# Loading and scaling in the front of a fused top-k attention and PReLU-MLP kernel: v cast on the way in, one scaling a tick, w_in turned in pieces

## The chip, the cores and the metric

The kernel runs on one core of one Trainium2 chip. The metric is the device time of one execution in microseconds; the time given for a kernel is the median of its runs. A core has five engines that run side by side, each with its own instruction stream: TensorE (PE, with its weight loads PEld), VectorE (DVE), ScalarE (ACT), GpSimd (POOL) and SyncE (SP, which here issues DMAs only). They wait for one another through semaphores. DMAs are issued by SyncE, GpSimd or ScalarE, in the order of that engine's stream.

## The reference

```python
scores = scale * np.matmul(q, k.transpose(0, 1, 3, 2))          # 8 x 8 heads, 576 x 576, D = 64
kth = np.partition(scores, -32, axis=-1)[..., -32:-31]
scores = np.where(scores >= kth, scores, -1e9)
attn = softmax(scores)                                           # rows
x = (attn @ v) with the heads of a batch side by side            # 4608 x 512
h = x @ w_in                                                     # 512 x 2048
g = np.maximum(h, 0.0) + alpha * np.minimum(h, 0.0)
out = g @ w_out                                                  # 2048 x 512
```

All inputs and the output are float32.

## The kernel before

The work is cut into 32 pairs of heads (a pair shares the 128 partitions) and 288 tiles of 128 query rows by 576 keys, nine tiles to a pair (`TPP = 9`; the ninth holds the last 64 rows of both heads). Tiles are taken singly or two at a time ("units"); the ninth of a pair is a unit of its own.

The order of all instructions is written out by hand in one loop over ticks n (from line 837 of the kernel before; one tile's work per tick on each engine, spread over several ticks). Each tile goes through:

- `scores`: TensorE, q times k in float32 into PSUM (`ps`).
- `act_b`: ScalarE adds a per-row limit `NT0` to the scores (`b`); `act_s`: ScalarE sums the signs of b (`h`, `S_all`), which counts how many scores are over the limit; `act_e`: ScalarE takes the exponential.
- `side_of`: GpSimd turns the count of the tile before into a sign bit `SG`; `flip`: VectorE applies it to b (`y`). The flip of tile n - 1 stands at the end of VectorE's tick n.
- `seg_ops` and `merge_ops`: VectorE finds the largest of six segments of y and merges them (`C`, `L`), from which `sel_*` and `limit` pick the exact limit `KP`.
- `mask` (VectorE, `mk`) and `weights` (GpSimd, `w`), seven ticks behind the scores; then SyncE issues a DMA that turns the weights (`wT`), and TensorE multiplies them with v (`av`, `pu`), after which VectorE takes reciprocals (`av_rz`, `rz`).

On GpSimd a tick is: a possible weight load, the weights product of the tile seven ticks back, then the sign of tile n - 1. On VectorE the mask comes first and the flip last.

`prep_plan(p)` gives each pair its preparation: the turning of q and k by TensorE (`pq`, `pk`, `pt`), their copies out of PSUM by ScalarE, a statistic of the scores (`pg`, `GK`, `pr`, `P`, `st`, `M2`) that ends in `NT0`, and `act_v`, the cast of v from float32 (`st_v`) to bfloat16 (`v_bf`) by ScalarE. For pair 0 it runs ahead of the loop at ticks -16 to -1, for pair 1 at ticks 0 to 9, with VectorE's part `dve_2` waiting for ScalarE's `act_m` at tick 7. `load` and `load_v` issue the loads of q, k and v; `load_v` uses SyncE.

`weight_steps` prepares the MLP beside the first tiles, one step a tick from a queue: alpha is loaded and turned; each 128-row block f of w_out (16 of them) is loaded into one of three staging buffers and scaled twice by ScalarE in one tick, by 1 - alpha into `w_out_b` (line 644) and by alpha into `lin(f)`, which borrows space in `xT` (line 645); w_in is loaded and cast by GpSimd's DMA in four parts kk (`w_in`, two issues each) and each part is turned by one SyncE DMA (`w_in2`, line 636); last, `w_id` multiplies the turned w_in with the scaled w_out (64 products of 128 x 512, line 653), so that the PReLU can be done as a ReLU and one more product. One f takes two ticks; all of it takes ticks 0 to 47. From tick 51 the same queue holds the MLP's own steps.

The pieces of a tick run in this order: the scores of the next unit, what ScalarE still owes from the last step (the scalings), b and h of this tile, one step of the queue, the preparation's TensorE part, then VectorE's and GpSimd's work.

## Time and profile before

| | us |
|---|---|
| median of 3 runs (872.99 to 875.49) | 873.02 |
| the profiled execution, its own time | 873.98 |
| span of the profiled execution | 872.1 |
| VectorE busy | 835.1 |
| ScalarE busy | 790.3 |
| TensorE busy | 721.9 |
| GpSimd busy | 431.0 |
| mean granted clock of TensorE | 0.943 |

In the rows of the timeline the columns are start and length in us, the engine, the line of the kernel, the operation, what it writes and reads with the shape, the number of instructions merged into the row, and in brackets the idle time of the engine just before and what ended it. In rows of stretches they are the stretch, its length, the busy time of PE, PEld, DVE, ACT and POOL with the number of instructions, the granted TensorE clock, the busy share of the DMA engines and GB/s. In grouped rows they are the busy time in us, the mean of one in ns, and the idle time before them.

### The profile page before, as it was taken

The page shows a single profiled execution, that of the slowest core. Times are in us where ns is not written, and L with a number is a line of the kernel's source. Part 1 is how long each engine was busy: PE and PEld are TensorE (multiplying, and loading weights), DVE is VectorE, ACT ScalarE, POOL GpSimd, SP SyncE. Part 2 cuts the span into 40 slices and gives each one's busy share as a digit, 9 for nine tenths or more (in the row PEclk, how much of TensorE's full clock was granted, in tenths as well). Part 3 has the DMA queues.
Part 4 walks back from the last instruction along what each step waited for, and adds up shares of the span by engine and source line. Part 5 has one row for each costly group of instructions (what it writes and reads, how often), then busy time and mean ns, then how long its engine had stood idle before and what let it go on. Part 6 is the DMA issues. An engine that isn't in the chain of part 4 may idle for free.

```text
span 872.1 us, 20608 instructions
## 1 busy us (share of the span) xinstructions
PE 721.9 (83%) x5697; PEld 428.3 (49%) x5771; DVE 835.1 (96%) x5188; ACT 790.3 (91%) x1873; POOL 431.0 (49%) x630
## 2 busy tenths in 40 slices
PE   6776688778978789787987789977897988899996
PEld 4443444334554345444454445643455554566674
DVE  4999999999999999999999999999999999999992
ACT  6999999999999999889999999989999899979861
POOL 1455545555454555545555455554554555544530
PEclk9997779899979999989998999989999999999999
DMA  7999644644665545564576445475455543535442
GB/s 161 156 178 199 131 89 90 126 91 97 135 139 107 108 102 116 100 135 95 114 154 115 98 97 116 111 136 98 92 128 121 121 103 81 106 71 100 91 96 56
DMA packets 342619, 99.37 MB, mean 114 GB/s; under 512 B 334672, under 2 KB 334944, under 8 KB 342496
## 3 DMA queue, kind: packets, MB, share of 16 engines
q1 hardware_dynamic: 340144, 95.58, 54.4%
q0 software_dynamic: 1152, 2.10, 2.0%
q8 instruction: 47, 0.77, 0.4%
q14 instruction: 76, 0.62, 0.2%
q10 hardware_dynamic: 1200, 0.30, 0.2%
HBM read 36.71 MB, written 9.44 MB: 53 GB/s over the span
## 4 chain that ended last, share of the span: by engine, by line
DVE 62%; ACT 21%; PE 12%; DMA 2%; issue 1%; POOL 1%; SPq 0%; DVEq 0%; another core or an unknown queue 0%; ACTq 0%
DVE C L369 20%; DVE y L359 9%; DVE mk L433 9%; DVE C L386 8%; DVE L L384 7%; ACT b L337 5%; ACT h L343 5%; ACT e L348 4%; PE ps L328 4%; PE pz L715 3%; PE ph L697 2%; ACT gT L703 2%; DVE P L246 2%; ACT xb L523 2%; PE pu L494 1%
## 5 line engine op out<-in xcount | busy, mean ns | idle before, releaser
L443 POOL TENSOR_TENSOR w<-mk,e 128x576 bf16<-128x576 bf16 x250 | 319.3, 1277 | 337.9 <-DVE mk L433 187.5
L369 DVE MAX8 C<-y 128x8 f32<-128x96 f32 x1728 | 419.1, 243 | 0.1
L328 PE MATMUL ps<-qkT 64*128 64x288 f32 (+1 forms) x1280 | 256.5, 474 | 35.1 <-ACT b L337 34.6
L337 ACT ACTIVATE b<-ps,NT 128x576 f32<-128x576 f32 x288 | 202.3, 761 | 3.1 <-PE ps L328 3.1
L343 ACT ACTIVATE h<-b 128x576 bf16<-128x576 f32 x288 | 202.9, 705 | 1.7
L697 PE MATMUL ph<-xT,w_in_b 128*128 128x128 bf16 (+2 forms) x997 | 150.4, 292 | 40.8 <-ACT gT L703 33.6
L328 PEld LDWEIGHTS ps<-qkT 64*128 64x128 f32 (+1 forms) x1280 | 134.3, 194 | 97.6 <-ACT b L337 59.8
L348 ACT ACTIVATE e<-b 128x1152 bf16<-128x1152 f32 (+1 forms) x158 | 174.2, 1102 | 0.0
L384 DVE MAX8 L<-C 128x8 f32<-128x48 f32 x864 | 162.6, 188 | 0.1
L359 DVE TENSOR_SCALAR y<-b,SG 128x576 int32<-128x576 int32 x288 | 147.0, 510 | 8.2 <-POOL SG L353 7.8
L433 DVE TENSOR_SCALAR mk<-b,KP 128x576 bf16<-128x576 f32 x282 | 143.6, 509 | 0.0
L715 PE MATMUL pz<-w_out_b,gT 128*128 128x512 bf16 x543 | 132.4, 380 | 1.2 <-issue 0.5
L697 PEld LDWEIGHTS <-w_in_b 128*128 128x128 bf16 x1024 | 80.4, 100 | 104.0 <-issue 79.6
L703 ACT ACTIVATE gT<-ph 128x512 bf16<-128x512 f32 x140 | 86.0, 621 | 28.1 <-PE ph L697 28.1
L386 DVE MATCH_REPLACE8 C<-L,C 128x48 f32<-128x48 f32 x576 | 108.3, 188 | 0.0
L715 PEld LDWEIGHTS <-gT 128*128 128x128 bf16 x560 | 51.6, 98 | 68.5 <-issue 14.0
L494 PE MATMUL pu<-v_bf,wT 128*128 128x65 bf16 (+1 forms) x1600 | 69.4, 198 | 14.4 <-DMA wT<-w 6.9
L494 PEld LDWEIGHTS <-wT 128*128 128x128 bf16 (+1 forms) x1600 | 65.2, 103 | 25.6 <-issue 10.2
L353 POOL TENSOR_SCALAR SG<-S_all 128x1 int32<-128x1 f32 x288 | 65.3, 227 | 18.9 <-ACT h L343 18.8
L443 POOL TENSOR_TENSOR wm<-mk,e 128x576 bf16<-128x576 bf16 x32 | 40.8, 1276 | 49.9 <-DVE mk L433 45.6
L343 ACT ACTIVATION_READ_ACCUMULATOR h<-b 128x1 f32 x288 | 62.8, 218 | 0.0
L523 ACT ACTIVATE xb<-pu,rz 128x64 bf16<-128x64 f32 x224 | 54.5, 369 | 0.0
(113 smaller groups left out, 728.1 us busy)
## 6 DMA issues: line engine op xcount, KB each, us to landing
out_dram<-o_sb SPq DMA_DIRECT2D x34, 256.0 KB, 2.3
st_q<-in_q_dram SPq DMA_DIRECT2D x64, 128.0 KB, 2.8
st_v<-in_v_dram SPq DMA_DIRECT2D x64, 128.0 KB, 2.6
kst<-in_k_dram SPq DMA_DIRECT2D x62, 128.0 KB, 2.6
w_stage<-in_moe_w_out_dram SPq DMA_DIRECT2D x16, 256.0 KB, 3.1
w_in_b<-in_moe_w_in_dram POOLq DMA_DIRECT2D x8, 256.0 KB, 6.4
wT<-w SPq DMA_TRANSPOSE x128, 3.3
st_q<-in_q_dram SPq DMA_DIRECT2D x32, 32.0 KB, 2.5
```

What stands on the lines that cost most here:

```text
L328: nc.tensor.matmul(o_, l_, r_, start=True, stop=True)
L337: nc.scalar.activation(t["b"].rearrange("p (a c) -> p a c", a=2), t["ps"], AF.Identity, bias=NT0[:, p * TPP + j:p * TPP + j + 1], scale=ON ...
L343: nc.scalar.activation(h, tiles[n]["b"], AF.Sign, accum_out=S_all[:, n:n + 1])
L348: nc.scalar.activation(e, tiles[n0]["bu"], AF.Exp, scale=scl)
L359: nc.vector.tensor_scalar(t["y"].bitcast(I32), t["b"].bitcast(I32), FLIP, SG[:, n:n + 1], ALU.bitwise_xor, ALU.bitwise_xor)
L369: return [lambda g=g: nc.vector.max(out=C[:, n % TPP, g, :], in_=t["y"][:, g * SEG:(g + 1) * SEG]) for g in range(NSEG)]
L384: ops.append(lambda r=r, src=src: nc.vector.max(out=L[:, 8 * r:8 * r + 8], in_=src))
L386: ops.append(lambda r=r, src=src: nc.vector.match_replace(out=C2, in_to_replace=L[:, 8 * r:8 * r + 8], in_values=src, imm_value=NEG))
L433: nc.vector.tensor_scalar(t["mk"], t["b"], row_limit(n), None, ALU.is_ge)
L443: nc.gpsimd.tensor_tensor(dst, t["mk"], t["e"], ALU.mult)
L697: nc.tensor.matmul(hold[f][:, i, :], w_in_b[:, kk, (f + i) * 128:(f + i + 1) * 128], xT[:, kk, c0:c0 + tb], start=(kk == 0), stop=(kk == N ...
L715: nc.tensor.matmul(pz[0:m], hold["gT"][:, f, r0:r0 + m], w_out_b[:, f, :], start=False, stop=(f == NFT - 1))
```

## The change

Only the front is touched; from about tick 50 the two kernels have the same instructions.

- v of pairs 0 and 1 is no longer loaded into `st_v` by SyncE and cast by ScalarE: GpSimd's DMA casts it on its way into `v_bf`. The four DMAs of pair 0 are issued at the start, those of pair 1 one at the end of each of ticks 8 to 11. `act_v` falls away for both pairs. Two memsets a buffer become wider, so that the padding rows are zero.
- `act_k` of pair 0, the copy of the turned k, is done by VectorE.
- alpha's load is issued behind the loads of pair 1, ahead of the weight steps; its turning and copying come one and two ticks earlier (ticks 0 and 1).
- The two scalings of a w_out block no longer share a tick. For f = 0 to 4 (ticks 2 to 6) GpSimd does the one by 1 - alpha, ahead of the sign in its stream, and ScalarE the one by alpha, a tick later. For f = 5 to 15 ScalarE does both, one a tick, with a tick free after them but for f = 10.
- w_in's four parts are loaded at ticks 4, 9, 14 and 19 (before: 3, 7, 11, 15), and each is turned in four pieces of 128 x 512, one a tick, from three ticks later on (before: one turn of 128 x 2048 each at ticks 6, 10, 14, 18).
- `w_id` starts four ticks later and then goes on with 6, 5 and 5 products a tick (before 4); its last step is at tick 48 (before 47).

```diff
-    def load_v(p):
+    def load_v(p, parts=range(4)):
         hA = 2 * p
-        st_v = st_vs[p % 2]
-        nc.sync.dma_start(st_v[:, 0:4, :], vf[hA, 0:512, :].rearrange("(c p) d -> p c d", p=128))
...
+        dst = v_bfs[p][:, :, 0:D] if p < 2 else st_vs[p % 2]
+        en = nc.gpsimd if p < 2 else nc.sync
+        moves = ((dst[:, 0:4, :], vf[hA, 0:512, :].rearrange("(c p) d -> p c d", p=128)),
+                 (dst[0:64, 4, :], vf[hA, 512:S, :]),
+                 (dst[64:128, 5, :], vf[hA + 1, 0:64, :]),
+                 (dst[:, 6:10, :], vf[hA + 1, 64:S, :].rearrange("(c p) d -> p c d", p=128)))
+        for i in parts:
+            en.dma_start(*moves[i])
...
         def act_k():
-            nc.scalar.copy(d["qkT"][:, 1, 0:512], d["pk"])
+            (nc.vector.tensor_copy if p == 0 else nc.scalar.copy)(d["qkT"][:, 1, 0:512], d["pk"])
...
-        def w_in2(kk):
-            nc.sync.dma_start_transpose(hold["inT"][:, kk, :, :], w_in_b[:, kk, :])
+        def w_in2(kk, i):
+            nc.sync.dma_start_transpose(wh["inT"][:, kk, 4 * i:4 * i + 4, :],
+                                        w_in_b[:, kk, 512 * i:512 * i + 512])
...
-        def w_out2(f):
-            ws = hold.pop(f)
-            nc.scalar.activation(w_out_b[:, f, :], ws, AF.Copy, scale=alpha1m[:, f:f + 1])
-            nc.scalar.activation(lin(f), ws, AF.Copy, scale=alpha_sb[:, f:f + 1])
+        def scale(f, one_m, pool=False):
+            dst, s = (w_out_b[:, f, :], alpha1m) if one_m else (lin(f), alpha_sb)
+            if pool:
+                nc.gpsimd.tensor_scalar(dst, wh[f], s[:, f:f + 1], None, ALU.mult)
+            else:
+                nc.scalar.activation(dst, wh[f], AF.Copy, scale=s[:, f:f + 1])
...
+        ins = {4 + 5 * kk: (lambda kk=kk: w_in(kk)) for kk in range(NKT)}
+        more = {7 + 5 * kk + i: (lambda kk=kk, i=i: w_in2(kk, i))
+                for kk in range(NKT) for i in range(4)}
...
+        yield (lambda: (alpha1(), w_out(0), w_out(1))), alpha2
         yield (lambda: None), None
-        yield (lambda: (alpha1(), w_out(0), w_out(1))), alpha2
-        for f in range(NFT):
-            yield ((lambda f=f: (w_out(f + 2) if f + 2 < NFT else None,
-                                 w_in(f // 2) if f < 8 and f % 2 == 0 else None)),
-                   (lambda f=f: w_out2(f)))
-            yield ((lambda f=f: w_id(0, min(done[0] + 2, f)) if f >= 6 else None),
-                   (lambda f=f: w_in2(f // 2) if f < 8 and f % 2 == 1 else None))
+        k_ = 2
+        for f in range(5):
+            yield ((lambda f=f, k_=k_: (w_out(f + 2), scale(f, True, True), put_in(k_))),
+                   (lambda f=f: scale(f, False)))
+            k_ += 1
+        for f in range(5, NFT):
+            yield ((lambda f=f, k_=k_: (w_out(f + 2), put_in(k_))),
+                   (lambda f=f: scale(f, True)))
+            yield ((lambda f=f, k_=k_: (w_id(0, min(done[0] + 2, f) if k_ > 12 else 0),
+                                        put_in(k_ + 1))),
+                   (lambda f=f: scale(f, False)))
+            k_ += 2
+            if f % 6 != 4:
+                yield (lambda k_=k_: put_in(k_)), None
+                k_ += 1
         yield (lambda: w_id(0, NFT)), (lambda: w_id2(0))
         for kk in range(1, NKT):
-            for lim in (4, 8, 12, 16):
+            for lim in (6, 11, 16):
...
         load(0, nc.scalar)
         load(1)
+        load_alpha()
...
         load_v(0)
-        load_v(1)
...
+            if 8 <= n < 12:
+                put(n, "end", lambda i=n - 8: load_v(1, [i]))
```

More of the change, by code (lines that the diff above doesn't have):

```diff
@@ L607, in last_pz, with load_alpha @@
             nc.sync.dma_start(out[o0:o0 + 128, cs], o_sb[:, 0:256])
-    def weight_steps():
-        hold = {}
-        def alpha():
-            a16 = mlp.tile([128, DM], FP32, name="a16", tag="stage", bufs=3)[0:NFT, 0:128]
-            nc.sync.dma_start(a16, moe_alpha.rearrange("(t p) -> t p", p=128))
-            hold["a16"] = a16
+    wh = {}
+    def load_alpha():
+        a16 = mlp.tile([128, DM], FP32, name="a16", tag="stage", bufs=3)[0:NFT, 0:128]
+        nc.sync.dma_start(a16, moe_alpha.rearrange("(t p) -> t p", p=128))
+        wh["a16"] = a16
+    def weight_steps():
         def alpha1():
             aps = ps_m.tile([128, NFT], FP32, name="aps", tag="misc")
-            nc.tensor.transpose(aps, hold["a16"], ident_f[0:NFT, 0:NFT])
-            hold["aps"] = aps
-            hold["inT"] = mlp.tile([128, NKT, NFT, 128], BF16, name="w_inT", tag="gT", bufs=1)
+            nc.tensor.transpose(aps, wh["a16"], ident_f[0:NFT, 0:NFT])
+            wh["aps"] = aps
+            wh["inT"] = mlp.tile([128, NKT, NFT, 128], BF16, name="w_inT", tag="gT", bufs=1)
         def alpha2():
-            nc.scalar.copy(alpha_sb, hold["aps"])
+            nc.scalar.copy(alpha_sb, wh["aps"])
             nc.gpsimd.tensor_scalar(alpha1m, alpha_sb, -1.0, 1.0, ALU.mult, ALU.add)
```

34 lines of the change are left out of this document (18 added, 16 removed).

## The prediction

> **What bounds the kernel now.** I read the page's busy line first, then busy time by stretches, then the waits and the timeline of the engine that comes out as the bound.
>
> ```profile
> PE 721.9 (83%) x5697; PEld 428.3 (49%) x5771; DVE 835.1 (96%) x5188; ACT 790.3 (91%) x1873; POOL 431.0 (49%) x630
> ...
> 0.00:20.00 20.00, 13.82 (x66) 9.49 (x66) 7.60 (x76) 12.28 (x28) 3.60 (x24) 1.00 0.72 164
> 20.00:80.00 60.00, 42.39 (x249) 25.08 (x251) 57.56 (x354) 59.29 (x132) 29.88 (x46) 0.95 1.04 176
> 80.00:125.00 45.00, 35.28 (x221) 20.23 (x222) 43.06 (x268) 43.12 (x99) 22.56 (x32) 0.69 0.63 125
> 125.00:400.00 275.00, 225.45 (x1742) 127.42 (x1764) 275.00 (x1718) 259.07 (x635) 143.90 (x203) 0.94 0.55 110
> ```
>
> VectorE is busy 835.1 of 872.1 us, and from 125 to 400 without a gap (third engine figure). The change takes next to nothing from VectorE, so the time can only fall by VectorE's idle time, and only by what lies in the front, where the change is: 12.4 us before 20, 2.44 from 20 to 80, 1.94 from 80 to 125. Their places on VectorE's timeline (idle time and its end in brackets):
>
> ```profile
> 14.17 0.52 DVE L359 TENSOR_SCALAR y<-b,SG 128x576 int32<-128x576 int32 x1 [3.54 <-POOL SG L353]
> 20.39 0.52 DVE L359 TENSOR_SCALAR y<-b,SG 128x576 int32<-128x576 int32 x1 [2.41 <-POOL SG L353]
> 31.46 0.17 DVE L271 TENSOR_TENSOR sq<-M,sq 128x9 f32<-128x9 f32 x1 [0.60 <-ACT M L267]
> 79.30 0.18 DVE L511 RECIPROCAL rz<-pu 128x4 f32<-128x4 f32 x1 [1.10 <-PE pu L494]
> 118.37 0.69 DVE L246 TENSOR_TENSOR P<-pr,qkT 128x512 bf16<-128x512 f32 x1 [1.88 <-PE pr L238]
> ```
>
> Five waits: two for the first flips (tiles 0 and 2), one for pair 1's statistics, and two of TensorE, 1.10 at 79 and 1.88 at 118. I take them in turn; I number ticks by the main loop.
>
> **The start.** ScalarE and TensorE, in order of time:
>
> ```profile
> 8.54 0.59 ACT L212 COPY qkT<-pk 128x512 f32<-128x512 f32 x1 [1.44 <-PE pk L208]
> 9.18 2.29 PE L328 MATMUL ps<-qkT 64*128 64x288 f32 x8 [0.28 <-ACT qkT L212]
> 11.07 0.73 ACT L203 CAST v_bf<-st_v 128x640 bf16<-128x640 f32 x1 [1.72 <-DMA st_v<-in_v_dram]
> 11.71 1.37 ACT L337 ACTIVATE b<-ps,NT 128x576 f32<-128x576 f32 x2
> 12.96 0.68 ACT L343 ACTIVATE h<-b 128x576 bf16<-128x576 f32 x1
> 13.77 0.68 ACT L343 ACTIVATE h<-b 128x576 bf16<-128x576 f32 x1
> 14.45 0.57 ACT L200 COPY qkT<-pq 128x512 f32<-128x512 f32 x1
> 20.60 0.71 ACT L644 ACTIVATE w_out_b<-w_stage,alpha1m 128x512 bf16<-128x512 f32 x1
> 21.21 0.71 ACT L645 ACTIVATE xT<-w_stage,alpha_sb 128x512 bf16<-128x512 f32 x1
> 25.18 0.59 ACT L200 COPY qkT<-pq 128x512 f32<-128x512 f32 x1 [0.35 <-PE pq L197]
> ```
>
> Pair 0's v cast sits before the first b and waits for its DMA; without it the first b could go when the scores are there. Scores end at 9.18 + 2.29 = 11.47; the second b of the unit cannot start before, and the first h follows it by one b (12.96 - 11.71 = 1.25 for two, so 0.62): 11.55 + 0.62 = 12.17 against 12.96, a gain of 0.79. The copy of k moved to VectorE gains nothing by itself: VectorE is free after its P product, the nearest row (the 128x512 product out of PSUM, 0.69) is 0.1 longer than ScalarE's 0.59, and the statistics behind it start within 0.1 of before; I take 0, bounds -0.1 to +0.1. alpha is copied one tick earlier, same work.
>
> From there ScalarE sets the pace until pair 1's statistics (the 31.46 wait), since VectorE waits for h through GpSimd's sign. A scaling costs 0.61 (20.60 to 21.21). Up to that wait ScalarE had four scalings; now it has five (one a tick for f = 0 to 4): -0.61. They lie between two h's, where ScalarE lost 0.13 each time (h to h 0.81, h to another operation 0.68): three pairs, +0.4. The 0.35 wait at 25.18 goes (the transposes behind it do not move as far as the work ahead of it): +0.35. Sum 0.79 - 0.61 + 0.4 + 0.35 = 0.9 at 31.46. The flips of tiles 0 and 2 gain more (0.6 and about 2.4, the second because GpSimd no longer issues two w_in loads ahead of that sign), but what VectorE wins there it waits out at 31.46, for by then it would be 1.4 ahead of the statistics (ready at 31.46 - 0.60 = 30.86 before; 1.7 sooner now, the rest of the 2.4 being lost to a wait for pair 1's pr near 23; statistics at 30.5). That 1.4 also covers the five scalings given to GpSimd, each ahead of a sign: they cost between a short cast there and the 1.28 of a 576-wide product, and 1.4 holds one. Term: **-0.9** (bounds 0 to -1.5: all of the extra scaling on the path, or VectorE's full lead kept).
>
> **v of pair 1 on GpSimd, ticks 8 to 11.** VectorE's flip waits for the sign, which stands on GpSimd behind the weights product and now behind these issues:
>
> ```profile
> L632 POOL DMA_DIRECT2D w_in_b<-in_moe_w_in_dram x8 | 5.0, 624 | 0.0
> 36.31 1.27 POOL L443 TENSOR_TENSOR w<-mk,e 128x576 bf16<-128x576 bf16 x1 [1.60 <-DVE mk L433]
> 37.55 0.23 POOL L353 TENSOR_SCALAR SG<-S_all 128x1 int32<-128x1 f32 x1
> 38.79 0.51 DVE L359 TENSOR_SCALAR y<-b,SG 128x576 int32<-128x576 int32 x1
> ...
> 41.22 1.27 POOL L632 DMA_DIRECT2D w_in_b<-in_moe_w_in_dram  x2
> ...
> 45.33 1.28 POOL L443 TENSOR_TENSOR w<-mk,e 128x576 bf16<-128x576 bf16 x1 [1.21 <-DVE mk L433]
> 46.57 0.23 POOL L353 TENSOR_SCALAR SG<-S_all 128x1 int32<-128x1 f32 x1
> 47.01 0.52 DVE L359 TENSOR_SCALAR y<-b,SG 128x576 int32<-128x576 int32 x1
> ...
> 6.51 0.59 SPq L150 DMA_DIRECT2D st_v<-in_v_dram  x1
> 7.15 0.51 SPq L151 DMA_DIRECT2D st_v<-in_v_dram  x1
> q0 software_dynamic: 1152, 2.10, 2.0%
> ```
>
> Room in tick 9: 1.60 before the product, and 38.79 - 37.78 = 1.01 behind the sign: 2.61. Room in tick 12: 1.21 + (47.01 - 46.80) = 1.42. Into the first go v's first part (512 rows) and, in the new order, a w_in pair (2 x 0.62 = 1.25); into the second v's last part. The small parts, 64 rows each, find about the same room as the last and fit. Price of a 512-row issue: at least 0.62, a whole w_in issue; at most by rows, 0.62 x (512 + 16)/144 = 2.3, where 144 is 1152 packets over 8 issues. At 0.62 nothing stalls. At 2.3: 2.3 + 1.25 - 2.61 = 0.94, and 2.3 - 1.42 = 0.88, together 1.8. SyncE's own issues of these very loads grow only from 0.51 (64 rows) to 0.59 (512), so I lean to the low end, 1.3, and enter **+0.4** (0 to 1.8). Pair 0's four are issued when GpSimd has nothing else, before its first sign at 13.9.
>
> **w_in turned in sixteen pieces; SyncE's queue.** The 1.10 at 79 is a TensorE wait for the turned weights of tile 12, which SyncE issued late, at 75.07:
>
> ```profile
> 42.73 7.15 SPq L636 DMA_TRANSPOSE w_inT<-w_in_b  x1
> 57.80 3.99 SPq L636 DMA_TRANSPOSE w_inT<-w_in_b  x1
> 71.87 2.16 SPq L636 DMA_TRANSPOSE w_inT<-w_in_b  x1
> 75.07 1.33 SPq L456 DMA_TRANSPOSE wT<-w  x1
> 154.00 5.17 SPq L557 DMA_TRANSPOSE xT<-xb  x4
> ```
>
> SyncE's queue was busy nearly without a gap from 42.7 to 75, three whole turns in it: 7.15 + 3.99 + 2.16 = 13.3. A piece has the shape of the xT turn, 5.17/4 = 1.29. Two pieces go ahead of tile 1's weights into a gap; nine stand between it and tile 12's: 11.6. So 1.7 less, and two w_out loads fewer in that stretch (they were issued earlier; 0.5 each): 2.7 earlier. Needed are 1.10 plus the 0.9 by which VectorE now runs ahead, 2.0. Term: **-1.1**, lost again (0) if a piece costs more than (13.3 + 1.0 - 2.0)/9 = 1.37. Counted with a queue that itself starts that 0.9 earlier, the point is 1.47. Pieces stretched as the longest whole turn, 7.15/4 = 1.79, would be over it.
>
> **Fewer scalings a tick.** The 1.88 at 118 is ScalarE's lateness handed on:
>
> ```profile
> 109.91 0.25 ACT L343 ACTIVATION_READ_ACCUMULATOR h<-b 128x1 f32 x1
> 110.92 0.52 DVE L359 TENSOR_SCALAR y<-b,SG 128x576 int32<-128x576 int32 x1
> 114.93 2.28 PE L328 MATMUL ps<-qkT 64*128 64x288 f32 x6 [0.47 <-ACT b L337]
> ...
> L653 PE MATMUL pl<-xT,w_inT 128*128 128x512 bf16 x45 | 12.6, 402 | 1.0 <-ACT w_id_b L658 0.7 <-issue 0.3
> ```
>
> At tile 33 h ends at 110.16 and its flip starts 0.76 later: ScalarE has no lead left. Then TensorE waits for b and VectorE for TensorE, at a granted clock of 0.69 in that stretch. By that tick ScalarE had done 30 scalings; now 23 and one v cast less: 7 x 0.61 + 0.61 = 4.9 earlier, of which VectorE's own 2.0 is used up; some 3 us of lead remain, over the 1.88. Term: **-1.9** (0 if TensorE at a lower clock is late by itself). Scaling now ends four ticks later, and the w_id products run 5 or 6 a tick in place of 4: 1.33 x 0.28 (12.6/45) = 0.37 a tick more for nine ticks, against TensorE's gap of 18% of a 2.9 us tick (225.45 of 275; 835.1/288), 0.5. It fits; without that cover up to 9 x 0.37 = 3.3, less the lead of 3. I enter 0.
>
> **The sum.** -0.9 + 0.4 - 1.1 - 1.9 = -3.5. The profiled execution took 873.98 (span 872.1 and 1.9 around it), so 870.5; it is 0.96 over the median of 873.02, so I forecast a median of **869.5 us**.
>
> **Rivals.**
> 1. *The v issues are dear* (a row's worth each, rather than an issue's worth). For it: a row has its own packet. Against: SyncE's 0.51 and 0.59. The term is 1.8 in place of 0.4: 870.9. *Or they are held up by VectorE*: an issue follows a sign, as the flip and then the mask do; were it kept waiting through both (0.51 + 0.51 at most), the large ones would stall (2.3 + 1.0 + 1.25 - 2.61) + (2.3 + 1.0 - 1.42) and the small ones 0.2 each, together 4.2: 873.3, a little slower than before. Against: a w_in pair behind the sign of tile 9 took 1.27 (row 41.22), in a tick that has its flip and mask like any other, and the mean of all eight is 0.62. The Trainium skill (SBUF — State Buffer, section on the two separate sides) has this as a rule: GpSimd cannot write its descriptors during a two-port fast-mode operation of VectorE, 620 ns alone becoming 3100 overlapped. By that figure the same rooms give, as an estimate, 1.7 for each large part and 1.7 for each small one, some 876.
> 2. *A TensorE wait stays*: the clock of 0.69 by itself makes TensorE late at 118, or a piece costs 1.5 to 1.8. One wait back: 870.6 or 871.4; both, 872.5.
> 3. *SyncE's queue becomes the bound* (slower). Sixteen issues have a floor each; if the w_in loads stretch them as they stretched the whole turns (7.15 against 2.16), tile 12's weights come 9 x (c - 1.47) late for a piece of c, and VectorE stands that long behind TensorE: 869.5 plus that. Slower than before begins where it passes 3.5, at c = 1.86; at c = 2.2 it is 6.6: 876.1. For it: 7.15 and 3.99. Against: the xT turns at 1.29.
> 4. *The front gains nothing*, ScalarE's extra scaling eats the 0.79 and nothing else moves: 873.
>
> **How the numbers follow.** Forecast (868.5 to 870.4) 0.43; better still, VectorE's lead partly kept, 0.05; rival 1 dear 0.13, held up 0.06; rival 2 0.16; rival 3 0.12; rival 4 0.05. A change of 0.3%, 2.6 us, is about what a measurement of this kernel can tell from none. Faster than 870.4: the forecast and the better case, 0.48. Slower than 875.6: most of rival 3 and a little of the held-up issues, 0.11. Between: 0.41. The range 868.0 to 874.5 leaves out most of rival 3 and the tail of the better case; the likeliest case's own is 868.5 to 870.4.
>
> **What would show it.** Right: first h near 12.2; VectorE's wait for pair 1's M ends near 30.5 and is about 1.4 long; the issues of v on GpSimd near 1.3 and no flip waiting for a sign in ticks 9 to 12; w_in pieces near 1.3 on SyncE's queue; no VectorE wait for pu near 79 nor for pr near 118, busy share 1 from 31 to 125. Wrong: v issues of 2 us and more with flips behind them, pieces over 1.5 with TensorE waiting for wT, or waits of VectorE for TensorE in ticks 40 to 48.

## The result, and the profile after

The changed kernel is slower: 876.99 us (median of 9 runs, 875.08 to 879.96) against 873.61 for the kernel before beside it (9 runs, 872.88 to 875.49); the ratio is 1.0035, 95% interval 1.0019 to 1.0051. Run again later it had 876.72 against 873.10, 1.0041 (1.0025 to 1.0056). Forecast were 869.5, with 868.0 to 874.5 as the range.

| | before | after |
|---|---|---|
| median beside each other, us | 873.61 | 876.99 |
| profiled execution, its own time | 873.98 | 876.06 |
| its span | 872.1 | 874.3 |
| mean granted TensorE clock | 0.943 | 0.911 |

The two clocks are those of one execution each. Three later profiles of what is all but the kernel before (the last three of the long table below) have 0.919 to 0.923, and 0.64 to 0.70 from 20 to 80 us, where the first one has 0.95; so the lower clock after is not put down to the change.

The page of the changed kernel, busy time of each engine, and below it the four stretches (PE, PEld, DVE, ACT, POOL, then granted clock, DMA share, GB/s):

```profile
PE 721.3 (83%) x5696; PEld 428.7 (49%) x5771; DVE 837.3 (96%) x5189; ACT 784.9 (90%) x1865; POOL 444.1 (51%) x643
```

```profile
0.00:20.00 20.00, 10.58 (x71) 7.09 (x71) 10.75 (x86) 12.12 (x28) 10.75 (x31) 0.97 0.73 144
20.00:80.00 60.00, 39.39 (x226) 23.24 (x228) 56.05 (x343) 55.19 (x126) 36.12 (x52) 0.59 0.99 165
80.00:125.00 45.00, 34.17 (x225) 20.30 (x229) 42.18 (x259) 40.11 (x92) 21.69 (x31) 0.69 0.72 138
125.00:400.00 275.00, 227.64 (x1742) 129.14 (x1771) 274.80 (x1721) 260.50 (x638) 144.12 (x204) 0.94 0.56 110
```

VectorE is still the bound. From 125 to 400 it works all but without a gap (274.80 of 275), so what was lost was lost in the front and at the very end. Before 20 VectorE was busy 3.2 us longer (10.75 against 7.60), but from 20 to 80 1.5 less and from 80 to 125 0.9 less. Its waits of a quarter of a microsecond and more from 12 on, from VectorE's timeline after:

```profile
13.51 0.52 DVE L363 TENSOR_SCALAR y<-b,SG 128x576 int32<-128x576 int32 x1 [2.83 <-POOL SG L357]
15.88 0.94 DVE L363 TENSOR_SCALAR y<-b,SG 128x576 int32<-128x576 int32 x1 [0.75 <-POOL SG L357]
...
27.80 0.52 DVE L363 TENSOR_SCALAR y<-b,SG 128x576 int32<-128x576 int32 x1 [0.72 <-POOL SG L357]
...
63.96 0.82 DVE L248 TENSOR_TENSOR P<-pr,qkT 128x512 bf16<-128x512 f32 x2 [1.36 <-PE pr L240]
...
81.93 0.18 DVE L515 RECIPROCAL rz<-pu 128x4 f32<-128x4 f32 x1 [3.49 <-PE pu L498]
...
93.64 0.82 DVE L248 TENSOR_TENSOR P<-pr,qkT 128x512 bf16<-128x512 f32 x2 [0.31 <-PE pr L240]
...
119.95 0.82 DVE L248 TENSOR_TENSOR P<-pr,qkT 128x512 bf16<-128x512 f32 x2 [0.58 <-PE pr L240]
```

The waits of the front are shorter, the one at 118 has shrunk from 1.88 to 0.58, but the one for pu near 80 has grown from 1.10 to 3.49 instead of going, and one of 1.36 for pr is new. TensorE's row and SyncE's queue, both after, say what stood behind the 3.49:

```profile
81.16 0.73 PE L498 MATMUL pu<-v_bf,wT 128*128 128x65 bf16 x10 [5.70 <-DMA wT<-w]
```

```profile
50.92 1.77 SPq L640 DMA_TRANSPOSE w_inT<-w_in_b  x1
...
63.85 1.66 SPq L640 DMA_TRANSPOSE w_inT<-w_in_b  x1
65.61 1.54 SPq L460 DMA_TRANSPOSE wT<-w  x1
67.23 3.60 SPq L140 DMA_DIRECT2D st_q<-in_q_dram  x2
...
73.52 1.29 SPq L640 DMA_TRANSPOSE w_inT<-w_in_b  x1
...
75.53 1.20 SPq L640 DMA_TRANSPOSE w_inT<-w_in_b  x1
76.83 1.30 SPq L460 DMA_TRANSPOSE wT<-w  x1
```

Tile 12's weights are issued at 76.83; before it was 75.07. The nine pieces between tile 1's weights and tile 12's took 12.9 us (1.24, 1.19, 1.33, 1.77, 1.66, 1.57, 1.66, 1.29, 1.20), and the load of pair 4 in front of them held the queue for 3.60 + 0.68 + 1.08 + 0.63 = 6.0 where it was 3.5.

To compare kernels over the whole length I use the start of the row in which VectorE takes the largest limit of a group of nine tiles (M written from C; 32 such rows, one for each group, the same work ahead of each). In the kernel before group 0's starts at 49.58, group 2's at 102.31, group 3's at 129.92 and group 31's at 852.22. Each other profile as a difference to that (minus is sooner), with the ratio of its times to those of the kernel before run beside it, and the time from the end of VectorE's last copy to the end of the span (6.2 before):

| kernel | ratio (95% interval) | group 0 | group 2 | group 3 | group 31 | end |
|---|---|---|---|---|---|---|
| changed | 1.0035 (1.0019 to 1.0051) | -1.17 | +2.88 | +1.58 | +0.67 | 7.7 |
| changed, again | 1.0041 (1.0025 to 1.0056) | -0.31 | +2.58 | +1.29 | +0.07 | 7.8 |
| changed, whole turns | 0.9994 (0.9980 to 1.0008) | -0.13 | -0.16 | -1.89 | -0.80 | 7.5 |
| the same, again | 0.9992 (0.9978 to 1.0006) | -0.32 | -0.47 | -2.21 | -3.92 | 6.6 |
| changed, v as before | 1.0057 (1.0035 to 1.0078) | +2.65 | +6.04 | +4.09 | +1.93 | 7.5 |
| changed, no scaling on GpSimd | 1.0055 (1.0035 to 1.0074) | +2.82 | +6.77 | +4.80 | +4.27 | 6.8 |
| changed, pieces spread | 1.0016 (0.9998 to 1.0035) | -0.22 | +0.68 | -1.30 | -1.61 | 7.7 |
| before with pieces | 1.0039 (1.0022 to 1.0055) | -0.36 | +2.80 | +1.07 | -0.56 | 7.8 |
| changed, w_in loaded sooner | 1.0012 (0.9996 to 1.0029) | +0.45 | +1.20 | -0.78 | -0.79 | 7.8 |
| whole turns, TensorE busy early | 0.9968 (0.9948 to 0.9987) | -0.98 | -0.72 | -2.47 | -1.62 | 6.6 |
| whole turns, scaling late | 0.9980 (0.9964 to 0.9996) | -2.01 | -2.12 | -3.78 | +0.15 | 6.1 |
| both | 0.9974 (0.9955 to 0.9993) | -3.35 | -3.35 | -4.78 | -2.33 | 6.2 |
| before with v alone | 1.0002 (0.9985 to 1.0018) | -0.30 | +0.65 | -0.41 | -1.24 | 6.3 |
| before, TensorE busy early | 1.0003 (0.9986 to 1.0021) | -0.17 | +0.85 | +0.84 | -1.74 | 6.2 |
| before, 12 loads more | 1.0007 (0.9990 to 1.0024) | -0.33 | +0.66 | -1.34 | -1.11 | 7.4 |
| before, 4 loads more | 1.0011 (0.9997 to 1.0025) | -0.11 | +0.28 | +0.34 | -1.76 | 6.1 |

One profile is one execution: the kernels that are the kernel before but for a trifle (the last three) differ from it by up to 1.3 at group 3 and are 1.1 to 1.8 sooner at group 31. Two executions of one program (whole turns) lie 3.1 apart at group 31. So I read places and lengths of waits from the profiles and gains from the ratios.

### The profile page after: what moved, and what is told of

It is laid out like the page before. It is cut to its first block, busy times and chain, and to the rows that moved or that the text cites. A ratio compares the mean times of both kernels' runs of the same rounds, so it can differ in the third digit from the quotient of the medians.

```text
span 874.3 us, 20623 instructions
## 1 busy us (share of the span) xinstructions
PE 721.3 (83%) x5696; PEld 428.7 (49%) x5771; DVE 837.3 (96%) x5189; ACT 784.9 (90%) x1865; POOL 444.1 (51%) x643
## 3 DMA queue, kind: packets, MB, share of 16 engines
q0 software_dynamic: 3584, 2.39, 2.5%
## 4 chain that ended last, share of the span: by engine, by line
DVE 69%; ACT 15%; PE 11%; DMA 2%; issue 1%; POOL 1%; SPq 0%; DVEq 0%; POOLq 0%
DVE C L373 23%; DVE y L363 10%; DVE mk L437 10%; DVE C L390 8%; DVE L L388 8%; ACT b L341 4%; ACT h L347 3%; PE ps L332 3%; ACT e L352 3%; PE pz L740 2%; DVE P L248 2%; PE ph L722 2%; ACT gT L728 2%; ACT xb L527 1%; DVE L L407 1%
## 5 line engine op out<-in xcount | busy, mean ns | idle before, releaser
L347 ACT ACTIVATION_READ_ACCUMULATOR h<-b 128x1 f32 x288 | 62.9, 218 | 0.0
```

Source lines behind the costliest of these rows:

```text
L347: nc.scalar.activation(h, tiles[n]["b"], AF.Sign, accum_out=S_all[:, n:n + 1])
```

## The experiments

My theory Q was that SyncE's queue brings tile 12's weights late. Its rivals were the traffic of the casting loads (D), TensorE's clock (C) and GpSimd's scalings (G). Four kernels, each with one part of the change undone or moved.

**Whole turns of w_in in the changed kernel.**

```diff
-            nc.sync.dma_start_transpose(wh["inT"][:, kk, 4 * i:4 * i + 4, :],
-                                        w_in_b[:, kk, 512 * i:512 * i + 512])
+            if i == 3:
+                nc.sync.dma_start_transpose(wh["inT"][:, kk, :, :], w_in_b[:, kk, :])
```

> The changed kernel, with each part of w_in turned whole again, at the tick of what was its fourth piece. Theory Q (SyncE's queue: eleven pieces of 1.2 to 1.8 us and the loads stretched among them bring tile 12's turned weights late, and VectorE waits 3.49 for pu at 82): the wait at 82 falls to 2 or less and the median to 873 to 875. Rival D (it is the DMA traffic of the casting loads of v and w_in, not the pieces): the issue of tile 12's weights stays near 76.8, the wait near 3.5, the median 876 to 878. Rival C (TensorE's clock in 30 to 66 alone): no change, 876 to 878.

Measured 873.19 against 873.33, 0.9994 (0.9980 to 1.0008). Its waits on VectorE's timeline, all of them from 14 to 160, and rows of SyncE's queue:

```profile
14.49 0.95 DVE L363 TENSOR_SCALAR y<-b,SG 128x576 int32<-128x576 int32 x1 [3.81 <-POOL SG L357]
...
28.85 0.52 DVE L363 TENSOR_SCALAR y<-b,SG 128x576 int32<-128x576 int32 x1 [1.13 <-POOL SG L357]
...
64.49 0.82 DVE L248 TENSOR_TENSOR P<-pr,qkT 128x512 bf16<-128x512 f32 x2 [0.78 <-PE pr L240]
```

```profile
44.10 2.82 SPq L641 DMA_TRANSPOSE w_inT<-w_in_b  x1
...
57.49 2.97 SPq L641 DMA_TRANSPOSE w_inT<-w_in_b  x1
...
74.04 1.43 SPq L460 DMA_TRANSPOSE wT<-w  x1
75.58 2.46 SPq L641 DMA_TRANSPOSE w_inT<-w_in_b  x1
```

No wait is left at 82, and none at 118. Tile 12's weights go out at 74.04. Q holds; C falls (TensorE's clock from 20 to 80 is 0.64 here, 0.59 in the changed kernel), and the casting loads alone (D) do not bring the wait. A whole turn whose part has landed costs SyncE 2.5 to 3.0, the four together 10.7; sixteen pieces at 1.2 are 19.2. Part of the gain is also that only two turns (5.8) stand between tile 1's weights and tile 12's here, since the third was due behind them.

**v as before in the changed kernel**: loads on SyncE ahead of the loop, casts on ScalarE in their old ticks.

```diff
-        dst = v_bfs[p][:, :, 0:D] if p < 2 else st_vs[p % 2]
-        en = nc.gpsimd if p < 2 else nc.sync
+        dst = st_vs[p % 2]
+        en = nc.sync
...
         load_v(0)
+        load_v(1)
```

> The changed kernel, with v of pairs 0 and 1 loaded by SyncE and cast by ScalarE as before. Theory Q: the front's gain at the first flip (0.66) goes back and the waits at 64 and 82 stay: 877 to 878.5. Rival D: without the casting loads of v the stretched issues on SyncE (3.30 and 3.60 us) shrink, the wait at 82 is 1.5 or less, 873 to 875.

Measured 878.43, 1.0057 (1.0035 to 1.0078). D falls as far as v's casting loads go: the wait for pu is 3.63 at 84.44. The casting loads of w_in are still there; they are tested below. What v's move is worth shows elsewhere. SyncE's and GpSimd's rows of this kernel:

```profile
15.63 6.75 SPq L644 DMA_DIRECT2D w_stage<-in_moe_w_out_dram  x5
```

```profile
18.65 1.60 POOL L649 TENSOR_SCALAR w_out_b<-w_stage,alpha1m 128x512 bf16<-128x512 f32 x1 [4.07 <-DMA w_stage<-in_moe_w_out_dram]
```

With eight loads of v ahead of them (4.6 us of issuing), the first w_out loads start at 15.6; GpSimd's scaling waits 4.07 for them, and the sign for the flip of tile 1 stands behind that scaling. In the changed kernel they start at 10.90.

**No scaling on GpSimd in the changed kernel.**

```diff
-            yield ((lambda f=f, k_=k_: (w_out(f + 2), scale(f, True, True), put_in(k_))),
-                   (lambda f=f: scale(f, False)))
+            yield ((lambda f=f, k_=k_: (w_out(f + 2), put_in(k_))),
+                   (lambda f=f: (scale(f, True), scale(f, False))))
```

> The changed kernel, with the five scalings of GpSimd (1.6 us each, one flip beside it 0.94 in place of 0.52) put on ScalarE. Theory Q: the flip waits of ticks 1 and 5 (0.75 and 0.72) go, ScalarE is 5 x 0.61 = 3 us busier by tick 6, the waits at 64 and 82 stay: 876.5 to 878.5. Rival G (GpSimd's scalings hold VectorE up, and cost what the change loses): 874 to 875.5.

Measured 878.56, 1.0055 (1.0035 to 1.0074), group 0 2.82 later. G falls as the cause of the loss: the wait for pu stays, 3.17 at 85.12. With ten scalings in ticks 2 to 6 ScalarE is what VectorE waits for, and longest here:

```profile
34.38 0.17 DVE L273 TENSOR_TENSOR sq<-M,sq 128x9 f32<-128x9 f32 x1 [3.19 <-ACT M L269]
```

**Pieces spread: parts 1 to 3 on every second tick from 13 to 35.**

```diff
-        more = {7 + 5 * kk + i: (lambda kk=kk, i=i: w_in2(kk, i))
+        more = {(7 + i if kk == 0 else 5 + 8 * kk + 2 * i): (lambda kk=kk, i=i: w_in2(kk, i))
```

> The changed kernel, with the twelve w_in pieces of parts 1 to 3 put on every second tick from 13 to 35 in place of twelve of ticks 12 to 25 (they are needed only from tick 41). Theory Q: three or four pieces fewer stand ahead of tile 12's weights, which are issued at 74 or before; no wait over 1 at 82; the wait of 1.36 for pr at 64 stays; 871.5 to 874. Rivals D and C: the wait stays over 2.5, 876 to 878.

Measured 874.90, 1.0016 (0.9998 to 1.0035): a little over the 871.5 to 874 that I gave it. Tile 12's weights go out at 74.73, the wait for pu is 1.06 at 79.02, and one of 1.02 for pr at 91.44 is new. Fewer pieces ahead of tile 12 take most of the wait away, but not as much as whole turns.

The next four ask whether the pieces alone are the loss (P), or the later casting loads (L), and what the front is worth.

**Pieces alone, in the kernel before**, one a tick from the tick of the first whole turn.

```diff
-        def w_in2(kk):
-            nc.sync.dma_start_transpose(hold["inT"][:, kk, :, :], w_in_b[:, kk, :])
+        def w_in2(j):
+            kk, i = divmod(j, 4)
+            if 0 <= j < 16:
+                nc.sync.dma_start_transpose(hold["inT"][:, kk, 4 * i:4 * i + 4, :],
+                                            w_in_b[:, kk, 512 * i:512 * i + 512])
...
-                   (lambda f=f: w_out2(f)))
+                   (lambda f=f: (w_out2(f), w_in2(2 * f - 3))))
...
-                   (lambda f=f: w_in2(f // 2) if f < 8 and f % 2 == 1 else None))
+                   (lambda f=f: w_in2(2 * f - 2)))
```

> The kernel before, with only w_in turned in sixteen pieces, one a tick from the tick of the first whole turn. Theory Q1 (what makes SyncE late in the changed kernel is what stands right ahead of tile 12's weights: two pieces and the stretched load of pair 4, not pieces as such; sixteen at 1.3 are 21 us against 17.5 for the four whole turns, but none holds the queue for 7): 873 to 875. Rival P (pieces as such are the loss): 875.5 to 877.5, with a wait of 2.5 or more for pu near 80.

Measured 877.01 against 873.87, 1.0039 (1.0022 to 1.0055): the whole loss of the change, by this part alone. My Q1, that pieces as such are harmless, falls; P holds. VectorE's timeline and SyncE's queue:

```profile
81.89 0.18 DVE L511 RECIPROCAL rz<-pu 128x4 f32<-128x4 f32 x1 [4.08 <-PE pu L494]
```

```profile
55.82 3.96 SPq L456 DMA_TRANSPOSE wT<-w  x1
...
61.18 1.60 SPq L643 DMA_DIRECT2D w_stage<-in_moe_w_out_dram  x1
...
70.11 1.11 SPq L140 DMA_DIRECT2D st_q<-in_q_dram  x2
...
73.91 2.59 SPq L638 DMA_TRANSPOSE w_inT<-w_in_b  x2
...
77.25 1.24 SPq L456 DMA_TRANSPOSE wT<-w  x1
```

From pair 3's load to tile 12's weights SyncE needs 41.6 us (35.67 to 77.25), before 39.2 (35.92 to 75.07). Its eleven pieces in there take 14.6 against 13.3 for three whole turns, and other issues between them are held longer: a turn of weights 3.96 (2.34 before), a w_out load 1.60 (0.35). The load of pair 4 is short, 1.11.

**The casting loads of w_in sooner, in the changed kernel.**

```diff
-        ins = {4 + 5 * kk: (lambda kk=kk: w_in(kk)) for kk in range(NKT)}
+        ins = {3 + 4 * kk: (lambda kk=kk: w_in(kk)) for kk in range(NKT)}
```

> The changed kernel, with the casting loads of w_in issued at ticks 3, 7, 11 and 15 as before in place of 4, 9, 14 and 19. Theory L (the last casting loads, in flight near 67, stretch SyncE's load of pair 4 from 1.1 to 3.6 us): that load is issued in 1.5 or less, tile 12's weights 2 us sooner, the wait at 82 is 1.5 or less, 874 to 875.5. Rival P (the pieces' own transfers stretch it): the load stays over 2.5 and the median at 876 to 878.

Measured 875.22, 1.0012 (0.9996 to 1.0029). L holds for the load of pair 4, which is short again, and tile 12's weights go out 1.4 sooner:

```profile
68.25 1.15 SPq L140 DMA_DIRECT2D st_q<-in_q_dram  x2
...
75.40 1.29 SPq L460 DMA_TRANSPOSE wT<-w  x1
```

The wait for pu is 0.69 at 79.54. So two things add up on SyncE's queue in the changed kernel: the pieces, and the casting loads in flight beside pair 4's load. In this kernel, taking either away nearly ends the wait. In the kernel before, the pieces bring it without late casting loads (4.08 above).

**TensorE busy from the start, with whole turns.**

```diff
+        nc.vector.memset(w_out_b[:, 0, :], 0.0)
+        wu = ps_m.tile([128, 512], FP32, name="wu", tag="misc")
+        for _ in range(8):
+            nc.tensor.matmul(wu, w_out_b[:, 0, 0:128], w_out_b[:, 0, :], start=True, stop=True)
         plan(0)
```

> The changed kernel with whole turns of w_in, and eight products of a zeroed tile on TensorE while it waits for the first loads (their result is not used). Theory W (the first scores run at half rate, 2.29 us for eight, in all profiles but the one of the changed kernel, where they took 1.24): with TensorE kept busy from the start the scores take 1.3, the first flip is at 13.5 or before, the first group ends 1 us sooner, and the median falls from 873.2 to 872 to 872.6. Rival: the rate does not follow what TensorE did before, scores at 2.29, 873 to 873.5.

Measured 871.59 against 873.87, 0.9968 (0.9948 to 0.9987), the fastest of all: the first eight score products take 1.24, the first flip starts at 12.93, group 0 comes 0.98 sooner. W holds.

**All scalings on ScalarE, one a tick from tick 7, with whole turns.**

```diff
-        for f in range(5):
-            yield ((lambda f=f, k_=k_: (w_out(f + 2), scale(f, True, True), put_in(k_))),
-                   (lambda f=f: scale(f, False)))
-            k_ += 1
-        for f in range(5, NFT):
+        for k_ in range(1, 7):
+            yield (lambda k_=k_: put_in(k_)), None
+        k_ = 7
+        for f in range(NFT):
...
-            if f % 6 != 4:
-                yield (lambda k_=k_: put_in(k_)), None
-                k_ += 1
```

> The changed kernel with whole turns of w_in, no scaling on GpSimd, and all 32 scalings on ScalarE, one a tick from tick 7 to 38. Theory S (GpSimd's scalings stretch what VectorE does beside them, three flips 0.95 for 0.52 and a statistics row 0.53 for 0.16, and delay one flip by 1.13): no flip over 0.6, the first group ends 2 us sooner than with the scalings on GpSimd, and a wait for pr near 118 takes back up to 1.9: 870.5 to 873. Rival: ScalarE, with one scaling in each tick, is late as before and all is given back: 873 to 875.

Measured 872.03, 0.9980 (0.9964 to 0.9996). S holds: group 0 comes 2.01 sooner than before, 1.9 sooner than with the scalings on GpSimd, and the flips have their old length. The flip's row in the two kernels (least, median and longest duration in ns), first with scalings on GpSimd (the changed kernel), then without:

```profile
L363 DVE TENSOR_SCALAR y<-b,SG x288: 457/510/945, 13.5 to 843.1; 128x576 int32<-128x576 int32 x144
```

```profile
L363 DVE TENSOR_SCALAR y<-b,SG x288: 459/511/599, 14.5 to 842.6; 128x576 int32<-128x576 int32 x144
```

Part of it is given back, as expected, though not at 118: in waits for pu, 1.03 at 68.83 and 1.55 at 130.62.

The next four put the two gains together, look at the changed kernel once more, and take two parts of the front by themselves. First the edits of the last two runs in one kernel:

> The changed kernel with whole turns of w_in, all scalings on ScalarE from tick 7, and the eight products of a zeroed tile ahead of the first transposes. If the two gains lie in different places (start of the scores; VectorE's stretched rows and late flips), they add: first scores 1.24, first flip near 13, first group 3 us sooner than before the change, 870 to 871.5. If ScalarE's scalings at 35 to 45 ticks are the next bound, it takes the sooner start back: 871.5 to 872.5.

Measured 871.53 against 873.10, 0.9974 (0.9955 to 0.9993). Group 0 comes 3.35 sooner and group 3 4.78, so in the front they add; of that 2.33 are left at group 31. The times do not tell it apart from the run with whole turns and the early products alone.

**The changed kernel, once more.**

> The changed kernel unchanged, profiled once more. Theory W: the first scores of the profile on record (1.24 us for eight) were the exception; here 2.29, first flip at 14.4 to 14.5, first group within 0.4 of before. The wait for pu near 82 is 2.5 or more again. Median 876 to 878. If the scores take 1.24 again, half rate is not the rule in this kernel and the front's gain is real.

Measured 876.72, 1.0041 (1.0025 to 1.0056). Its first scores, and those of the profile on record, with the b behind them; first the profile on record, then this one:

```profile
9.47 1.24 PE L332 MATMUL ps<-qkT 64*128 64x288 f32 x8 [0.44 <-DVE qkT L214]
...
10.78 1.37 ACT L341 ACTIVATE b<-ps,NT 128x576 f32<-128x576 f32 x2 [1.38 <-PE ps L332]
```

```profile
9.24 2.29 PE L332 MATMUL ps<-qkT 64*128 64x288 f32 x8 [0.38 <-DVE qkT L214]
...
11.56 1.37 ACT L341 ACTIVATE b<-ps,NT 128x576 f32<-128x576 f32 x2 [2.33 <-PE ps L332]
```

The same program does both. At 2.29 the first flip starts at 14.30, later than the 14.17 of before, and group 0 comes only 0.31 sooner. The wait for pu is 3.80 at 81.63. The one for pr at 64 is not there: in this execution TensorE had its full clock from 60 to 64 (1.00, against 0.50 in the profile on record), and pr started at 61.92 instead of 63.28.

**v's move alone, in the kernel before** (`load_v`, the zeroed rows of `v_bf`, pair 1's issues in ticks 8 to 11, no casts of pairs 0 and 1 on ScalarE).

```diff
+            if 8 <= n < 12:
+                put(n, "end", lambda i=n - 8: load_v(1, [i]))
```

> The kernel before, with only the loads of v of pairs 0 and 1 moved to GpSimd's casting DMA. Theory F (the first b waits for all eight products of its unit, not for the cast alone): first b at 11.5 to 11.6, first h at 12.8, a gain of 0.1 to 0.2 in place of the 0.79 that the prediction has; in all 873 to 874. Rival, the prediction's step: first h at 12.2, 872.3 to 873. If the issues of pair 1 on GpSimd hold flips up: 874 to 875.

Measured 873.31 against 873.10, 1.0002 (0.9985 to 1.0018), no change in time. Its profile fell on an execution with the scores at 1.24, and there the first b starts at 10.91 and the first h at 12.17, so it cannot show the 11.5 that I expected at 2.29; the time says that the move alone wins nothing. What the first b waits for here is its limit `NT0`, which VectorE starts to write at 10.63: a third bound, 0.6 below the other two. Although both the cast and the slow scores are out of the way in this execution, group 0 comes only 0.30 sooner, no more than in the last two kernels of the long table, which leave the front alone (0.11 and 0.33).

**The early products alone, in the kernel before** (the same four lines as above).

> The kernel before, with only the eight products of a zeroed tile ahead. Theory F: the scores take 1.24, but ScalarE's cast of v, whose load lands at 11, holds the first b at 11.7 as before: first flip 14.0 to 14.2, 873 to 874. Rival (the full rate alone gives the gain of the run with whole turns): first flip at 13.2, 872 to 873.

Measured 873.24, 1.0003 (0.9986 to 1.0021). Rows of the start:

```profile
8.65 1.24 PE L328 MATMUL ps<-qkT 64*128 64x288 f32 x8
10.91 0.73 ACT L203 CAST v_bf<-st_v 128x640 bf16<-128x640 f32 x1 [1.91 <-DMA st_v<-in_v_dram]
11.54 1.37 ACT L337 ACTIVATE b<-ps,NT 128x576 f32<-128x576 f32 x2
```

Theory F holds: the scores are there at 9.9, and the cast of v, waiting for its load, holds the first b to 11.54 (11.71 before). The start has two bounds at the same height, the cast and the scores at half rate. Taking one away wins nothing in the median. With both away the changed kernel gains 0.7 to 0.9 at group 0 (the profile on record against the second one, and whole turns with the early products against without). In the kernel before, the one profile with both away did not gain at group 0, so the rest of the changed front has a part in it; the two edits together were not timed there.

The last three ask about the end of the span. The waits explain a smaller loss than the medians show, and in most of the profiles with pieces the time from VectorE's last copy to the end is longer. Twelve loads more in the kernel before, then four (204 for 212), and the change with whole turns unchanged:

```diff
+            if 200 <= n < 212:
+                put(n, "end", lambda i=4 * (n - 200): nc.sync.dma_start(
+                    pad[:, i:i + 4], moe_alpha.rearrange("(t p) -> t p", p=128)[0:1, 0:4]))
```

> The kernel before, with twelve loads of 16 bytes added to SyncE's queue at ticks 200 to 211, where it has room (what they load is not used). Theory E (twelve more transfers in SyncE's stream lengthen the end by a fetch of instructions): from VectorE's last copy to the end 7.5 to 7.8 in place of 6.2, median 1 to 1.5 over before. Rival: 6.1 to 6.3 as before, median within 0.5 of before; the longer end has another cause.

> The same with four such loads. Theory E, if a fetch brings a block and the threshold lies between 4 and 12: 6.2 and the median of before; if it lies below 4: as with twelve. Rival: 6.2.

> The changed kernel with whole turns of w_in, run a second time. If the length of the end is the program's: 7.5 from the last copy to the end again; if it is the execution's: often 6.2. Median 872.5 to 874 and no wait for pu or pr over 1.2 from 70 to 125 in either case.

With twelve loads more the end is 7.4, with four 6.1. That speaks for E, by one profile each. But twelve is not the changed kernel's number: with its twelve more pieces and v's eight loads gone from SyncE, that has 611 DMAs on SyncE's queue against 607 before, four more, and four more gave 6.1 here. With whole turns it has 599, fewer than before, and 7.5 all the same. The end goes better with the packets on the queue that the profile calls q14 instruction:

```profile
q14 instruction: 76, 0.62, 0.2%
...
q14 instruction: 78, 0.64, 0.2%
```

The columns are packets, MB and the share of the DMA engines' time; the first row is the kernel before, the second the changed one. Over the seventeen profiles the end is 6.1 to 6.8 with 76 packets, 6.6 to 7.8 with 77 (twelve loads more has 77, four 76) and 7.7 to 7.8 with 78. So a longer end goes with more fetching of instructions, of the whole program and not of SyncE's transfers alone; no run sets the number of packets and nothing else. The times are less clear: 874.18 and 873.40 against 872.61, ratios 1.0007 (0.9990 to 1.0024) and 1.0011 (0.9997 to 1.0025), neither told from none. The change with whole turns had 7.5 the first time and 6.6 the second, both with 77 packets, so the length is not the program's alone. Its time is 872.27, 0.9992 (0.9978 to 1.0006), as the first time, and it has no wait of a quarter of a microsecond or more from 70 to 125.

## Why the prediction was wrong, by its own steps

**SyncE's queue (forecast -1.1; measured +2.4): the step that failed.** The wait for pu went from 1.10 to 3.49 (3.80 in the second profile; in the last three kernels of the table, which leave this queue alone, it is 1.04 to 2.15). The place was that of rival 3, the mechanism too, the price was not: it put the loss on pieces of 2.2 us, and they took 1.43 on average, at the break-even of 1.37 to 1.47 that the prediction itself gave. The sum was wrong in what it held fixed. It moved the issues of SyncE as blocks of their old length. The pieces came out at 12.9 for 11.6 (+1.3), and the load of pair 4 at 6.0 for 3.5 (+2.5), for w_in's last casting loads, issued 10 us later than before (62.9 against 52.9), were in flight beside it. These make up 3.8 of the 4.5 between the 2.7 sooner of the forecast and the 1.8 later of the trace. The runs bear out both: pieces alone in the kernel before cost the whole loss (1.0039), the change without them is level (0.9994, 0.9992), and with the casting loads where they were the change costs 1.0012, which is not told from none. Two rivals had a figure near the measured time, some 876 each: rival 3 for pieces of 2.2 us, rival 1 for the dearest issues on GpSimd. That the time fell there is chance, as neither price came true.

**The front (forecast -0.9; measured at group 0 -1.2 in one profile, -0.1 to -0.3 in four with the same front).** The number looked right and was not. The prediction let the first b start while the last products of its unit still ran, and the first h follow at 12.17. In every profile the first b starts after all eight products, and those take 2.29 in all but those in which TensorE ran at full rate. So the cast of v was one of two bounds (11.54 with the cast alone, 11.56 to 11.77 with the scores alone), and the 0.79 was worth 0 without the other. The first h at 12.17 came about once, with v's move alone, and there only because the scores took 1.24. The copy of k on VectorE, entered at 0 with bounds of 0.1, cost between nothing and 0.3: from TensorE's first transposes to its first scores it is 4.41 before (4.77 to 9.18), 4.43 and 4.52 in the two profiles of the changed kernel and 4.65 with whole turns (4.78 to 9.43). Two prices were missing for GpSimd's scalings: they take 1.6 each, over the upper bound of 1.28, and stretch VectorE's rows beside them. What the front did win is the room for w_out's loads on SyncE, by v's move: without it group 0 is 3 later.

**v of pair 1 on GpSimd (forecast +0.4; measured 0).** The mechanism holds and the size lies within its bounds. GpSimd's rows in the changed kernel:

```profile
33.57 0.83 POOL L156 DMA_DIRECT2D v_bf<-in_v_dram  x1
34.40 1.07 POOL L636 DMA_DIRECT2D w_in_b<-in_moe_w_in_dram  x2
...
42.81 1.01 POOL L156 DMA_DIRECT2D v_bf<-in_v_dram  x1
```

0.83 and 1.01 for the large parts, not 1.3, 0.59 and 0.70 for the small ones, and no flip waits in ticks 9 to 12. Both forms of rival 1 are out.

**Fewer scalings a tick (forecast -1.9; measured -1.3, and -1.9 with whole turns).** It came out about as forecast, but no run changes the scalings alone, and the wait at 118 is a poor witness. It is 0.58 in the changed kernel and gone with whole turns. It is gone too in the kernel before with pieces, where ScalarE has its two scalings a tick as ever and VectorE stands 4.08 at 82; and in the kernel with twelve loads more, which changes nothing before tick 200, it stood at 91 instead:

```profile
91.45 0.82 DVE L247 TENSOR_TENSOR P<-pr,qkT 128x512 bf16<-128x512 f32 x2 [1.14 <-PE pr L239]
```

So the wait at 118 also goes where VectorE is held earlier. That ScalarE's lead helped is borne out only by whole turns, where VectorE is held neither at 82 nor at 118, and there together with the other parts of the change.

**w_id at 5 or 6 a tick (forecast 0).** Wrong by 1.4 in one execution and by nothing in the other. The prediction asked whether the products fit into TensorE's gap, not what stands behind them. TensorE's rows, before and after:

```profile
60.63 1.24 PE L328 MATMUL ps<-qkT 64*128 64x288 f32 x6 [0.34 <-ACT b L337]
61.80 0.44 PE L238 MATMUL pr<-qkT,GK 64*64 64x512 bf16 x4
62.17 0.60 PE L653 MATMUL pl<-xT,w_inT 128*128 128x512 bf16 x2
```

```profile
60.09 2.29 PE L332 MATMUL ps<-qkT 64*128 64x288 f32 x6 [0.30 <-ACT b L341]
62.31 1.03 PE L662 MATMUL pl<-xT,w_inT 128*128 128x512 bf16 x2
63.28 0.69 PE L240 MATMUL pr<-qkT,GK 64*64 64x512 bf16 x4
```

Two w_id products now come ahead of pr in that tick, and in this execution all of it runs at half rate (granted clock 0.50 from 60 to 64); VectorE waits 1.36 (0.78 with whole turns). The order and the low clock both have a part in it: in the second profile of the changed kernel TensorE had its full clock there and VectorE did not wait, and in the kernel before with four loads more it had 0.51, with pr ahead of the w_id products, and VectorE did not wait either.

**The sum.** On VectorE in the profile on record: -1.17 at group 0, +1.36 at 64, 3.49 - 1.10 = +2.39 at 82, +0.31 at 93, 0.58 - 1.88 = -1.30 at 119, together +1.59; group 3 comes 1.58 later. The prediction made the sum -3.5. The medians differ by 3.4 to 3.6. Against the three kernels that are nearly the kernel before (1.1 to 1.8 sooner than its profile at group 31), the two profiles of the change are 1.2 to 2.4 late at group 31, and their end is 1.5 longer than the 6.2 of before (one of the three has 7.4 too); that comes to 2.7 to 3.9. By that estimate, from five executions, 1.2 to 2.4 of the median's loss arise on VectorE, where the wait for tile 12's weights outweighs what the front and 118 won, and about 1.5 at the end. That the pieces cause the loss is shown by the times, from both sides; that they bring the wait at 82 is shown by the traces. How the loss divides between that wait and the end is not shown, and what makes the end longer stays open: it goes with the number of instruction packets, not with the number of DMAs on SyncE, and it changes from execution to execution. Open too is why whole turns, 1.9 and 2.2 sooner at group 3 than the profile before, are level in the median.

## What to carry to other kernels

Cutting a turn in four cost the issuing queue 1.6 to 1.9 times as much (1.2 us a quarter, 2.5 to 3.0 the whole, with its data there); before cutting a transfer, look at what stands behind it on that queue, and at which transfers will be in flight beside the ones it passes. When an engine's wait has two bounds of the same height, removing one wins nothing, and a profile in which the other is low by chance shows a gain that the median does not have. A second profile of the same program is worth more than a finer reading of the first.

## What the runs showed of the hardware

**TensorE's rate at the start differed between executions, and was the full one whenever TensorE had been kept busy.** The first eight score products took 2.29 in twelve of the fourteen profiles without early products, and 1.24 in the changed kernel's profile on record and in the run with v alone; with eight products of zeros ahead they took 1.24 all three times. The granted clock of the profile does not show it: it is 1.00 from 0 to 20 before, where they took 2.29, and 0.97 after, where they took 1.24. The Trainium skill (TensorE: Matmul & The Clock Gate, Part 1: The HAM clock gate) says that the array starts at half rate and goes to full rate after a window of some 3.4 us in which it was busy, and that the window runs freely, so that the same kernel changes over at different points. The runs agree: one program had both lengths, and after the early products, which kept TensorE busy for 3.2 to 3.6 us, the first transposes took 0.63 in one kernel and still 1.09 in another (1.09 without them), but the scores 1.24 in both.

**VectorE's flip was slowed by GpSimd's scaling, without waiting for its end.** GpSimd's row in the changed kernel, beside which the flip at 15.88 ran:

```profile
15.82 1.59 POOL L651 TENSOR_SCALAR w_out_b<-w_stage,alpha1m 128x512 bf16<-128x512 f32 x1
```

The flip took 0.94 for 0.52 and ended at 16.82, 0.6 ahead of the scaling (17.41). What counts is when the flip starts: flips that began up to 0.1 after a scaling did took 0.91 to 0.97 (15.88 and 20.89 here, 14.30 and 18.75 in the second profile), one that began 0.22 after it 0.78 (16.27 in the second profile), and one that began 0.65 after it 0.50, the usual length (18.52 here, beside the scaling of 17.87 to 19.48). The slowed ones all ended about 1.0 after the scaling's start. The Trainium skill (SBUF — State Buffer, SBUF: two separate sides) has the port that the two engines share as an exclusive lock: where VectorE's operation needs it, by a two-port mode for one, whichever of the two starts first holds it for its whole instruction and the other is fully blocked. Here the flip was stretched by 0.42 and not held to 17.41; no run shows in which mode it runs. GpSimd's spans are rough, so this is told of the flip's length above all.
